# Performer attention and a GEGLU block on one core: the maximum of the k rows as a factor on v instead of a subtraction, and the k projection as row-tiled pairs

## The chip, the cores and the metric

One core of one Trainium2 chip runs the whole program. The metric is device microseconds of one execution. The kernel before took 423.97 us (median of 3 runs, 422.4 to 424.92).

Names used below: PE is the matrix engine, DVE the vector engine, ACT the scalar (activation) engine, POOL the GpSimd engine, SP the engine that issues most DMA transfers. PSUM is the accumulator memory that PE writes.

## The reference, cut to what matters

There are 64 heads (8 batches of 8), 576 tokens each, 64 wide, and 128 random features. The result of attention goes through a GEGLU feed-forward block (512 to 1536 to 512).

```python
def phi(x):                                   # x: q or k, scaled
    proj = np.einsum('bhsd,md->bhsm', x, omega)
    h = proj - np.sum(x * x, axis=-1, keepdims=True) / 2.0
    h = h - np.max(h, axis=-1, keepdims=True)
    return np.exp(h) / np.sqrt(m)
q_p, k_p = (phi(q_s), phi(k_s))
kv  = np.einsum('bhsm,bhsd->bhmd', k_p, v)
z   = np.sum(k_p, axis=2)
num = np.einsum('bhsm,bhmd->bhsd', q_p, kv)
den = np.einsum('bhsm,bhm->bhs', q_p, z)[..., None] + 1e-06
return num / den
# ... then gelu(x @ w_gate) * (x @ w_val) @ w_out
```

Two facts of this arithmetic matter. The maximum of a q row cancels in num / den (but for the 1e-06), so the kernel leaves it out. The maximum of a k row does not cancel: every k row s is weighted by exp(-max_s) before it is summed over s. That weight may be put on the row of k_p (by a subtraction before the exponential), or on the row of v and of the ones that make z (by a factor). The change goes from the first to the second.

## The kernel before

The batch loop interleaves attention of batch t+1 with the feed-forward work of token block t. Only the parts that the argument touches are shown.

```python
    def load_v(b):                      # two batches ahead; POOL casts fp32 to bf16
        vf = ld.tile([P, H, R * D], F32, name="vf", bufs=1)
        vrf = ld.tile([P, 4, D], F32, name="vrf", bufs=1)
        nc.sync.dma_start(out=vf, in_=v[b, :, :SM, :]...)
        ...
        nc.gpsimd.tensor_copy(ve[:, :, :, :D], vf.rearrange("p h (r d) -> p h r d", r=R))
        ...                             # v_ext / v_rbd: v with a column of ones, two buffers
    def attention(b):
        kT = transpose_main(k_in, "k")  # 16 PE transposes, one DVE copy
        ...
        def k_feat(ps, dst, n):
            nmax = work.tile([P, n, 1], F32, name="nmax", bufs=4)
            nc.vector.reduce_max(nmax, ps, axis=AX, negate=True)
            kd = work.tile([P, n, M], F32, name="kd", bufs=5)
            nc.vector.tensor_add(kd, ps, nmax.broadcast_to((P, n, M)))
            nc.scalar.activation(dst, kd, func=Exp)
        for hp in range(H // 2):
            pk = att_tile([P, 8, M], F32, "pk")
            for i in range(4):          # omega2T: block diagonal, 128 x 256
                nc.tensor.matmul(pk[:, 2 * i:2 * i + 2, :], kT[:, 4 * hp + i, :], omega2T)
            k_feat(pk, k_p[:, 2 * hp:2 * hp + 2]..., 8)
        ...                             # the same for the 64 rest rows: pkr, k_pr
        qT = transpose_main(q_in, "q")
        for hp in range(H // 2):
            pq = att_tile([P, 2, 512], F32, "pq")
            ...                         # two 64-row matmuls of 512 columns
            nc.scalar.activation(q_pT[:, hp]..., pq, func=Exp)
        ...
        kz_ps = att_tile([P, 2, 512], F32, "kz_ps")
        for j in range(4):
            nc.tensor.matmul(kz_ps[...], k_pr[:, j, :], vr[:, j]..., start=True, stop=False)
            ...                         # 8 matmuls k_p x v_ext into the same bank
        kz = work.tile([P, 2, 4 * DP1], BF16, name="kz")
        nc.vector.tensor_copy(kz, kz_ps[:, :, :4 * DP1])
        ...                             # nd = q_p x kz, division, transposes into xT
    with tc.manual_schedule(engines={mybir.EngineType.Activation}):
        attention(0)
        for t in range(N_TOK):
            ...                         # loads of batch t + 2
            if t + 1 < B: attention(t + 1)
            if t > 0: project_out(t - 1)
            gate_val(t)
        project_out(N_TOK - 1)
```

ACT runs in the written order. The other engines' orders are chosen when the program is compiled, and then every engine runs its list strictly in order. PSUM is split: two buffers of two banks ("att") for all attention results, four of one bank ("mo") for the feed-forward.

The softmax here doesn't subtract the row's maximum and nothing guards it: scores larger than these inputs give would overflow.

## Time and profile before

| | before |
|---|---|
| span of the profiled run | 422.2 us |
| PE, DVE, ACT, POOL busy | 89%, 59%, 37%, 15% |
| start, until the k transposes of the third batch | 92.7 us |
| six steady iterations (92.69 to 344.59 us, each from its first k transpose to the next's) | 251.9 us, 41.85 to 42.46 us each; the last ends at the first o_ps matmul |
| tail without attention | 77.6 us |

The page's first and fourth parts: busy time with its share of the span and the number of instructions, and the chain of work that ended last, by engine.

```profile
PE 373.9 (89%) x2518; PEld 193.2 (46%) x2561; DVE 249.7 (59%) x380; ACT 154.6 (37%) x202; POOL 62.9 (15%) x87
PE 74%; ACT 9%; DVE 8%; DMA 4%; issue 2%; POOL 1%; SPq 0%; DVEq 0%; POOLq 0%
```

PE holds three quarters of the chain, so what counts is whether PE works and whether it waits. Next, groups of instructions of the kernel before: line, engine, operation, output<-inputs, shapes, count | busy us, mean ns of one | idle time just before them and what ended it.

```profile
L194 DVE TENSOR_REDUCE nmax<-pk 128x8 f32<-128x1024 f32 x32 | 37.6, 1217 | 4.2 <-PE pk L202 4.2
L196 DVE TENSOR_TENSOR kd<-pk,nmax 128x1024 f32<-128x1024 f32 x32 | 37.5, 1213 | 0.0
L197 ACT ACTIVATE k_p<-kd 128x1024 bf16<-128x1024 f32 x32 | 33.8, 1057 | 91.3 <-DVE kd L196 90.1
L202 PE MATMUL pk<-omega2T,kT 128*128 128x256 bf16 x128 | 19.8, 292 | 5.0 <-DVE kd L196 4.9
L104 POOL CAST v_ext_70<-vf 128x2048 bf16<-128x2048 f32 x4 | 7.6, 1892 | 0.6 <-DMA vf<-in_v_dram 0.4
```

The third line is tempting: ACT stood idle for 90 us ahead of the k exponential, waiting for the subtraction. But in the steady iterations PE fills that time with feed-forward matmuls (pk waits for DVE only 5 us in the whole run), so shortening it saves little directly. The last line is, beside the building of the identity matrix at the start, the only kind of arithmetic that POOL does in this kernel: a cast with one input, 1.89 us for 2048 elements per partition, done before anyone needs it.

The first and the last steady iteration in the windows view: the stretch, its length, busy time and count of PE, weight loads, DVE, ACT, POOL, then granted PE clock, DMA share and GB/s.

```profile
92.69:134.64 41.95, 41.01 (x299) 21.15 (x303) 29.51 (x44) 18.75 (x25) 6.95 (x9) 1.00 0.42 82
302.74:344.59 41.85, 40.65 (x297) 21.17 (x302) 29.17 (x44) 18.70 (x24) 0.00 (x0) 1.00 0.09 26
```

And PE in order of time where kz starts in the first of them (start, duration, instruction, count, idle time before it with its releaser):

```profile
111.95 0.59 PE L303 MATMUL v_ps<-xT,w_val_sb 128*128 128x512 bf16 x2
112.43 0.23 PE L231 MATMUL kz_ps<-v_rbd_72,k_pr 128*128 128x130 bf16 x1
...
114.82 0.38 PE L297 MATMUL g_ps<-xT,w_gate_sb 128*128 128x512 bf16 x1 [0.53 <-ACT g_gelu L300]
```

kz starts 19.7 us after the iteration's first k transpose, without any wait; shortly after it PE stands for 0.5 us, because ACT is still busy and no PSUM bank of the feed-forward is free.

### The profile page before, as it was taken

The page shows a single profiled execution, that of the slowest core. Times are in us where ns is not written, and L with a number is a line of the kernel's source. Part 1 is how long each engine was busy: PE and PEld are TensorE (multiplying, and loading weights), DVE is VectorE, ACT ScalarE, POOL GpSimd, SP SyncE. Part 2 cuts the span into 40 slices and gives each one's busy share as a digit, 9 for nine tenths or more (in the row PEclk, how much of TensorE's full clock was granted, in tenths as well). Part 3 has the DMA queues.
Part 4 walks back from the last instruction along what each step waited for, and adds up shares of the span by engine and source line. Part 5 has one row for each costly group of instructions (what it writes and reads, how often), then busy time and mean ns, then how long its engine had stood idle before and what let it go on. Part 6 is the DMA issues. An engine that isn't in the chain of part 4 may idle for free.

```text
span 422.2 us, 6222 instructions
## 1 busy us (share of the span) xinstructions
PE 373.9 (89%) x2518; PEld 193.2 (46%) x2561; DVE 249.7 (59%) x380; ACT 154.6 (37%) x202; POOL 62.9 (15%) x87
## 2 busy tenths in 40 slices
PE   0456847999999999998999999999999999999995
PEld 0224524555455545554555455545554544444442
DVE  1482593649574957495749574957595632433331
ACT  1043046243724362446243624472347221321320
POOL 7563523002301230112011300000000000000000
PEclk9999975999999999999999999999999999999999
DMA  9999997305730673067306600030003003003004
GB/s 179 233 224 207 204 225 85 104 0 64 150 113 2 62 152 112 0 64 149 113 0 64 151 0 3 0 102 2 0 2 99 2 2 100 0 2 99 0 8 93
DMA packets 48444, 33.46 MB, mean 79 GB/s; under 512 B 14624, under 2 KB 43808, under 8 KB 48416
## 3 DMA queue, kind: packets, MB, share of 16 engines
q0 software_dynamic: 30096, 14.16, 26.6%
q1 hardware_dynamic: 18320, 18.91, 15.4%
q8 instruction: 20, 0.33, 0.3%
q14 instruction: 8, 0.07, 0.0%
HBM read 37.78 MB, written 9.44 MB: 112 GB/s over the span
## 4 chain that ended last, share of the span: by engine, by line
PE 74%; ACT 9%; DVE 8%; DMA 4%; issue 2%; POOL 1%; SPq 0%; DVEq 0%; POOLq 0%
PE g_ps L297 21%; PE o_ps L327 20%; PE v_ps L303 19%; ACT q_pT L219 6%; DVE nmax L194 3%; DMA q_rest<-in_q_dram 3%; DVE kd L196 3%; PE pk L202 3%; PE nd L250 2%; PE qT_ps L169 2%; PE xt_ps L261 2%; PE kT_ps L169 2%; ACT L300 2%; DMA out_dram<-o_sb 1%; PE kz_ps L235 1%
## 5 line engine op out<-in xcount | busy, mean ns | idle before, releaser
L297 PE MATMUL g_ps<-xT,w_gate_sb 128*128 128x512 bf16 x422 | 115.7, 383 | 4.1 <-ACT g_gelu L300 2.5
L305 DVE TENSOR_TENSOR gated<-g_gelu,v_ps 128x512 bf16<-128x512 bf16 x108 | 73.7, 682 | 72.5 <-PE v_ps L303 65.7
L300 ACT ACTIVATE g_gelu<-g_ps 128x512 bf16<-128x512 f32 x108 | 63.7, 597 | 143.3 <-PE g_ps L297 138.4
L303 PE MATMUL v_ps<-xT,w_val_sb 128*128 128x512 bf16 x414 | 113.0, 382 | 2.4 <-DVE o_sb L330 1.2
L327 PE MATMUL o_ps<-w_out_sb,gated 128*128 128x512 bf16 x417 | 98.2, 379 | 0.7
L197 ACT ACTIVATE k_p<-kd 128x1024 bf16<-128x1024 f32 x32 | 33.8, 1057 | 91.3 <-DVE kd L196 90.1
L303 PEld LDWEIGHTS <-w_val_sb 128*128 128x128 bf16 x432 | 41.1, 99 | 49.1 <-issue 7.0
L327 PEld LDWEIGHTS <-gated 128*128 128x128 bf16 x432 | 41.8, 98 | 43.0
L297 PEld LDWEIGHTS <-w_gate_sb 128*128 128x128 bf16 x432 | 40.9, 98 | 42.7 <-issue 2.5
L330 DVE COPY o_sb<-o_ps 128x512 f32<-128x512 f32 x36 | 24.0, 683 | 29.2 <-PE o_ps L327 20.7
L194 DVE TENSOR_REDUCE nmax<-pk 128x8 f32<-128x1024 f32 x32 | 37.6, 1217 | 4.2 <-PE pk L202 4.2
L196 DVE TENSOR_TENSOR kd<-pk,nmax 128x1024 f32<-128x1024 f32 x32 | 37.5, 1213 | 0.0
L219 ACT ACTIVATE q_pT<-pq 128x1024 bf16<-128x1024 f32 x32 | 30.2, 1030 | 11.5 <-PE pq L217 11.5
L239 DVE CAST kz<-kz_ps 128x520 bf16<-128x520 f32 x8 | 5.6, 699 | 33.8 <-PE kz_ps L235 33.8
L202 PE MATMUL pk<-omega2T,kT 128*128 128x256 bf16 x128 | 19.8, 292 | 5.0 <-DVE kd L196 4.9
L255 DVE TENSOR_TENSOR x_sb<-nd,iden 128x512 bf16<-128x512 f32 x32 | 22.0, 688 | 0.6
L71 POOL DMA_DIRECT2D k_in<-in_k_dram x8 | 7.2, 906 | 79.5 <-PE rT_ps L182 78.5
L202 PEld LDWEIGHTS <-kT 128*128 128x128 bf16 x128 | 11.5, 103 | 14.7 <-DVE kd L196 11.3
L217 PE MATMUL pq<-qT,omegaT_111 64*128 64x512 bf16 x64 | 12.9, 436 | 5.5 <-DVE qT L172 2.6
L250 PEld LDWEIGHTS <-q_pT 128*128 128x128 bf16 x256 | 12.0, 104 | 9.0 <-issue 6.0
L161 DVE COPY xT<-xt_ps 128x1024 bf16<-128x1024 bf16 (+3 forms) x22 | 11.4, 543 | 6.1 <-PE xt_ps L261 5.7
L250 PE MATMUL nd<-kz,q_pT 128*128 128x65 bf16 x256 | 13.3, 203 | 1.5 <-DVE kz L239 1.0
(66 smaller groups left out, 260.1 us busy)
## 6 DMA issues: line engine op xcount, KB each, us to landing
vf<-in_v_dram SPq DMA_DIRECT2D x8, 1024.0 KB, 5.8
out_dram<-o_sb SPq DMA_DIRECT2D x40, 128.0 KB, 2.4
k_in<-in_k_dram POOLq DMA_DIRECT2D x8, 512.0 KB, 7.9
q_in<-in_q_dram POOLq DMA_DIRECT2D x8, 512.0 KB, 7.5
out_dram<-o_sb SPq DMA_DIRECT2D x16, 256.0 KB, 2.5
w_gate_sb<-in_moe_w_gate_dram POOLq DMA_DIRECT2D x3, 512.0 KB, 14.9
w_val_sb<-in_moe_w_val_dram POOLq DMA_DIRECT2D x3, 512.0 KB, 14.1
w_out_sb<-in_moe_w_out_dram POOLq DMA_DIRECT2D x3, 512.0 KB, 19.4
```

What stands on the lines that cost most here:

```text
L194: nc.vector.reduce_max(nmax, ps, axis=AX, negate=True)
L196: nc.vector.tensor_add(kd, ps, nmax.broadcast_to((P, n, M)))
L197: nc.scalar.activation(dst, kd, func=Exp)
L202: nc.tensor.matmul(pk[:, 2 * i:2 * i + 2, :], kT[:, 4 * hp + i, :], omega2T)
L219: nc.scalar.activation(q_pT[:, hp].rearrange("m a c p -> m a (c p)"), pq, func=Exp)
L250: nc.tensor.matmul(nd[:, h // 4, (h % 4) * DP1:(h % 4 + 1) * DP1], q_pT[:, h // 2, r2, 2 * (h % 2) + rp, :], kz_h(h))
L297: nc.tensor.matmul(g_ps, w_gate_sb[:, jm, fs], xT[:, jm, :], start=(jm == 0), stop=(jm == N_DM - 1))
L300: nc.scalar.activation(g_gelu, g_ps, func=Gelu)
L303: nc.tensor.matmul(v_ps, w_val_sb[:, jm, fs], xT[:, jm, :], start=(jm == 0), stop=(jm == N_DM - 1))
L305: nc.vector.tensor_mul(gated[:, jf, :], g_gelu, v_ps)
L327: nc.tensor.matmul(o_ps, gated[:, jf, qq * P:(qq + 1) * P], w_out_sb[:, jf, :], start=(jf == 0), stop=(jf == N_DFF - 1))
L330: nc.vector.tensor_copy(o_sb, o_ps)
```

## The change

Its intent: take the subtraction from DVE and let the k exponential read PSUM at once, without waiting for the maximum. The maximum is exponentiated separately (128 x 36 values) and multiplied into v and the ones on POOL. The k projection becomes pairs of matmuls with 64 rows each, which use the two halves of the array, in place of one matmul against a half-empty block-diagonal matrix. The fp32 tiles of v get a second buffer, because they now live until the multiply.

```diff
-        vf = ld.tile([P, H, R * D], F32, name="vf", bufs=1)
-        vrf = ld.tile([P, 4, D], F32, name="vrf", bufs=1)
+        vf = ld.tile([P, H, R * D], F32, name="vf")          # the pool's 2 buffers
+        vrf = ld.tile([P, 4, D], F32, name="vrf")
...
-        nc.gpsimd.tensor_copy(ve[:, :, :, :D], vf.rearrange(...))   # and two for the rest rows
...
-        def k_feat(ps, dst, n): ...    # reduce_max, tensor_add, exponential
         for hp in range(H // 2):
-            pk = att_tile([P, 8, M], F32, "pk")
+            pk = att_tile([P, 2, 4, M], F32, "pk")
             for i in range(4):
-                nc.tensor.matmul(pk[:, 2 * i:2 * i + 2, :], kT[:, 4 * hp + i, :], omega2T)
-            k_feat(pk, ...)
+                for r2 in range(2):
+                    sl = slice(r2 * D, (r2 + 1) * D)
+                    nc.tensor.matmul(pk[:, r2, i, :], kT[sl, 4 * hp + i, :], omegaT2[sl])
+            nc.scalar.activation(k_p[:, hp]..., pk..., func=Exp)
+            nc.vector.reduce_max(nmax[:, :, 4 * hp:4 * hp + 4], pk, axis=AX, negate=True)
...
         for hp in range(H // 2):       # q features
             ...
             nc.scalar.activation(q_pT[:, hp]..., pq, func=Exp)
+            if hp == 0:
+                wk = work.tile([P, 2, 18], F32, name="wk")
+                nc.scalar.activation(wk, nmax, func=Exp)
...
+        for hh in range(2):
+            isl = slice(8 * hh, 8 * hh + 8)
+            nc.gpsimd.tensor_mul(vei[:, isl, :, :D], vfi[:, isl],
+                                 wki[:, isl].unsqueeze(3).broadcast_to((P, 8, 2, D)))
+        nc.gpsimd.tensor_copy(vei[:, :, :, D], wki[:, :16])
+        for e in range(2):
+            ...                         # the rest rows: one multiply, one copy each
         kz_ps = att_tile([P, 2, 512], F32, "kz_ps")
```

The cut part re-indexes k_p and k_pr for the new order of rows.

More of the change, by code (lines that the diff above doesn't have):

```diff
@@ L88 @@
         nc.vector.memset(v_rbd[i], 0.0)
-        nc.vector.memset(v_ext[i][:, :, :, D:DP1], 1.0)
-        for e in range(2):
-            nc.vector.memset(v_rbd[i][e * SR:(e + 1) * SR, :, e, D:DP1], 1.0)
     def load_v(b):
-        vf = ld.tile([P, H, R * D], F32, name="vf", bufs=1)
-        vrf = ld.tile([P, 4, D], F32, name="vrf", bufs=1)
+        vf = ld.tile([P, H, R * D], F32, name="vf")
+        vrf = ld.tile([P, 4, D], F32, name="vrf")
         nc.sync.dma_start(
@@ L102, in load_v @@
                     .rearrange("j s d -> s j d"))
-        ve, vr = v_ext[b % 2], v_rbd[b % 2]
-        nc.gpsimd.tensor_copy(ve[:, :, :, :D],
-                              vf.rearrange("p h (r d) -> p h r d", r=R))
-        for e in range(2):
-            sl = slice(e * SR, (e + 1) * SR)
-            nc.gpsimd.tensor_copy(vr[sl, :, e, :D], vrf[sl])
-        return ve, vr
+        return vf, vrf
     omega_f = singles.tile([M, D], F32)
@@ L122 @@
     omegaT2 = singles.tile([2 * D, M], BF16)
-    omega2T = singles.tile([2 * D, 2 * M], BF16)
-    nc.vector.memset(omega2T, 0.0)
     for e in range(2):
@@ L127 @@
         nc.vector.tensor_copy(omegaT2[sl], omegaT_ps)
-        nc.vector.tensor_copy(omega2T[sl, e * M:(e + 1) * M], omegaT_ps)
     w_gate_sb = singles.tile([P, N_DM, d_ff], BF16)
@@ L176, in attention @@
         k_in, k_rest, q_in, q_rest = kq.pop(b)
-        ve, vr = vx.pop(b)
+        vf, vrf = vx.pop(b)
+        ve, vr = v_ext[b % 2], v_rbd[b % 2]
         kT = transpose_main(k_in, "k")
@@ L186, in attention @@
         nc.vector.tensor_copy(rT, rT_ps)
-        k_p = work.tile([P, H, R, M], BF16, name="k_p")
-        k_pr = work.tile([P, 4, M], BF16, name="k_pr")
-        def k_feat(ps, dst, n):
-            nmax = work.tile([P, n, 1], F32, name="nmax", bufs=4)
-            nc.vector.reduce_max(nmax, ps, axis=AX, negate=True)
-            kd = work.tile([P, n, M], F32, name="kd", bufs=5)
-            nc.vector.tensor_add(kd, ps, nmax.broadcast_to((P, n, M)))
-            nc.scalar.activation(dst, kd, func=Exp)
+        k_p = work.tile([P, H // 2, 2, 4, M], BF16, name="k_p")
+        k_pr = work.tile([P, 2, 2, M], BF16, name="k_pr")
+        nmax = work.tile([P, 2, 18], F32, name="nmax")
         for hp in range(H // 2):
-            pk = att_tile([P, 8, M], F32, "pk")
+            pk = att_tile([P, 2, 4, M], F32, "pk")
             for i in range(4):
-                nc.tensor.matmul(pk[:, 2 * i:2 * i + 2, :], kT[:, 4 * hp + i, :], omega2T)
-            k_feat(pk, k_p[:, 2 * hp:2 * hp + 2].rearrange("p h r m -> p (h r) m"), 8)
-        pkr = att_tile([P, 4, M], F32, "pkr")
-        for jj in range(2):
-            nc.tensor.matmul(pkr[:, 2 * jj:2 * jj + 2, :], rT[:, jj, :], omega2T)
-        k_feat(pkr, k_pr, 4)
+                for r2 in range(2):
+                    sl = slice(r2 * D, (r2 + 1) * D)
+                    nc.tensor.matmul(pk[:, r2, i, :], kT[sl, 4 * hp + i, :], omegaT2[sl])
+            nc.scalar.activation(k_p[:, hp].rearrange("p a i m -> p a (i m)"),
+                                 pk.rearrange("p a i m -> p a (i m)"), func=Exp)
+            nc.vector.reduce_max(nmax[:, :, 4 * hp:4 * hp + 4], pk, axis=AX, negate=True)
+        pkr = att_tile([P, 2, 4, M], F32, "pkr")
+        for jj in range(2):
+            for j2 in range(2):
+                sl = slice(j2 * D, (j2 + 1) * D)
+                nc.tensor.matmul(pkr[:, j2, jj, :], rT[sl, jj, :], omegaT2[sl])
+        nc.scalar.activation(k_pr, pkr[:, :, :2], func=Exp)
+        nc.vector.reduce_max(nmax[:, :, 16:], pkr[:, :, :2], axis=AX, negate=True)
         qT = transpose_main(q_in, "q")
@@ L225, in attention @@
         nc.scalar.activation(q_pTr.rearrange("m a c p -> m a (c p)"), pqr[:, :, :256], func=Exp)
+        vei = ve.rearrange("p h (c r) d -> p (h c) r d", r=2)
+        vfi = vf.rearrange("p h (c r d) -> p (h c) r d", c=2, r=2)
+        wki = wk.rearrange("p r i -> p i r")
+        for hh in range(2):
[4 more added lines that the diff above has]
+        for e in range(2):
+            sl = slice(e * SR, (e + 1) * SR)
+            vre = vr[sl, :, e, :].rearrange("p (a j) d -> p a j d", j=2)
+            nc.gpsimd.tensor_mul(vre[..., :D],
+                                 vrf[sl].rearrange("p (a j) d -> p a j d", j=2),
+                                 wki[sl, 16:].unsqueeze(3).broadcast_to((SR, 2, 2, D)))
+            nc.gpsimd.tensor_copy(vre[..., D], wki[sl, 16:])
         kz_ps = att_tile([P, 2, 512], F32, "kz_ps")
@@ L230, in attention @@
             g, c0 = j // 2, (j % 2) * 2 * DP1
-            nc.tensor.matmul(kz_ps[:, g, c0:c0 + 2 * DP1], k_pr[:, j, :],
+            nc.tensor.matmul(kz_ps[:, g, c0:c0 + 2 * DP1], k_pr[:, j % 2, j // 2, :],
                              vr[:, j].rearrange("p e c -> p (e c)"), start=True, stop=False)
@@ L235, in attention @@
                     nc.tensor.matmul(kz_ps[:, g, c0 + e * DP1:c0 + (e + 1) * DP1],
-                                     k_p[:, 2 * j + e, r, :], ve[:, 2 * j + e, r, :],
+                                     k_p[:, j, r % 2, 2 * e + r // 2, :], ve[:, 2 * j + e, r, :],
                                      start=False, stop=(e == 1 and r == R - 1))
```

## The prediction

> **What bounds it now.** The page: span 422.2 us, PE 89% busy, DVE 59%, ACT 37%, POOL 15%. PE holds 74% of the chain that ended last. Three stages: a start (0 to 71 us) in which attention 0 and 1 run one after the other with PE often idle; six steady iterations of 42.0 us (92.85 to 344.75 in the chain); a 77 us tail without attention, which the change leaves alone. A steady iteration is 144 feed-forward matmuls at 0.216 us (31 us), about 8.5 us of attention matmuls, and about 2 us of PE waits. The page puts idle of 90 us on the k exponential, "waiting for DVE kd", but ACT is off the critical path there: PE fills that time with o_ps matmuls.
>
> **Removed.** Per batch DVE loses the subtraction: 4 x 1.21 + 0.68 = 5.5 us (33 to 36% of its k phase and copies). The k exponential reads PSUM directly and runs beside the reduction, so the k phase, serial on DVE, shrinks from about 10.5 us to 5.2 us. POOL loses its casts (1.89 + 2 x 0.40 us), which ran ahead of need.
>
> **Moved.** k projection: 18 matmuls of 256 columns at 0.108 us become 18 row-tiled pairs of 128 columns. The pq pairs show that two 64-row matmuls share the time of one (four take 0.54 us), but also about 0.1 us around a group; the Trainium skill (TensorEngine Tiling (Array Packing), Key Properties) says that changing the tiling mode drains the engine. Net PE: 0 to -0.5 us per batch, no more.
>
> **Added.** POOL must now multiply v by exp(-max) after the exponential of the max, and before any kz matmul, since the first kz matmul reads the v rest that POOL writes last. The trace has only one-input casts on POOL (0.92 ns per element). The Trainium skill (GPSIMD Engine Reference, section 3.1) puts a two-input operation at about 2.6 cycles per element, 4497 ns for 2048. My estimate from it: 2 x 2.3 + 2 x 0.6 + three small copies at 0.2 = 6.3 us. No run shows it yet.
>
> **On the critical path.** Steady state, counted from the k transposes. Now kz starts at 19.7 us. After: PE work puts pq at about 13.0 us, the first q exponential ends at 14.2, the small exponential at 14.4, POOL at about 20.7. The compiled order of PE places only 5 gate/value matmuls before kz, against 14 now, so PE should stand about 3.5 us in front of kz, and the 9 matmuls (1.9 us) come later. The later waits (about 1 us) vanish. Sum: +2.2 us per iteration, 13 us for six. Start: about 5 us saved per k phase, given back by 6.3 us of POOL after the first q exponential; in attention 0 POOL is also held by weight transfers issued ahead of it (until 33 us now). Net about +1 us (-3 to +4).
>
> **Predicted**: 436 us, range 424 to 447. Faster by over 2%: 5%; within 2%: 29%; slower: 66%.
>
> **What would show it.** Windows of one iteration: length about 44.2 us; DVE falling by about 5.5 us, ACT unchanged, POOL rising from about 6.9 to about 10.5 us. Waits: PE or its weight loads at kz waiting for POOL's v_rbd, about 3.5 us in each iteration; POOL multiply of 128x1024 at about 2.3 us. pk groups on PE no dearer than before.
>
> **What would make it wrong.** POOL multiplying at the cast's rate (about 1 us per 1024): its chain would be 3.3 us, kz no longer late, and the kernel about 1% faster. POOL slower than estimated, or the granted clock falling after each stand of 3 to 4 us: 450 us. The start gaining its full 5 us per attention: 5 to 8 us less.

## The result, and the profile after

The changed kernel took 443.32 us (median of 4 runs, 440.86 to 446.52) beside 423.36 us for the kernel before (4 runs). The ratio is 1.0472, with a 95% interval of 1.038 to 1.0564: slower. A ratio here is the mean time of one kernel's fast runs over that of the other's fast runs of the same rounds, so it is not quite the ratio of the medians. The four runs fall in two pairs, near 441 us (granted clock 0.965) and near 446 us (0.953 and 0.954); the profiled one, of 446.52 us, is of the second kind.

The same two parts of the page, after:

```profile
PE 377.6 (85%) x2660; PEld 193.4 (43%) x2705; DVE 210.4 (47%) x331; ACT 154.0 (35%) x210; POOL 85.5 (19%) x119
PE 21%; issue 9%; POOL 1%; DVE 0%; POOLq 0%
```

The second line warns of the chain view: it covers only a third of the span. The chain runs back from the last instruction to a POOL multiply, and there it is lost: the profile does not see what POOL waited for and calls it "issue". The waits view says the same:

```profile
POOL v_ext_71 L226 <- issue: 45.5, 4, 39.5
PE kz_ps L241 <- POOL v_rbd_73 L235: 11.9, 4, 3.4
PE kz_ps L241 <- POOL v_rbd_72 L235: 11.8, 4, 3.4
DVE nmax L190 <- ACT k_p L188: 4.3, 4, 2.0
```

(Columns: us in total, times, the longest.) What POOL waits for there is ACT, which writes the small exponential wk: in the iteration shown below wk ends at 108.84 us and the multiply starts at 108.98. "issue" hides that. The second and third lines are new and certain: at kz, eight times out of eight, PE waits for POOL, 23.7 us in all.

The groups after:

```profile
L190 DVE TENSOR_REDUCE nmax<-pk 128x8 f32<-128x1024 f32 x32 | 37.6, 1217 | 4.3 <-ACT k_p L188 4.3
L188 ACT ACTIVATE k_p<-pk 128x1024 bf16<-128x1024 f32 x32 | 31.9, 1022 | 62.4 <-PE pk L187 61.9
L187 PE MATMUL pk<-omegaT_102,kT 64*128 64x128 bf16 x256 | 12.3, 228 | 3.6 <-DVE nmax L190 3.6
L226 POOL TENSOR_TENSOR v_ext_71<-vf,wk 128x1024 bf16<-128x1024 f32 x8 | 15.3, 1928 | 45.5 <-issue 45.5
```

The subtraction is gone. POOL's multiply takes 1.93 us for 1024 elements, as long as its cast took for 2048. Here is what that does to one iteration: first POOL, then PE, in order of time.

```profile
108.98 3.82 POOL L226 TENSOR_TENSOR v_ext_70<-vf,wk 128x1024 bf16<-128x1024 f32 x2 [1.96 <-issue]
112.75 0.32 POOL L228 CAST v_ext_70<-wk 128x32 bf16<-128x32 f32 x1
112.92 0.61 POOL L232 TENSOR_TENSOR v_rbd_72<-vrf,wk 64x256 bf16<-64x256 f32 x1
...
114.32 0.20 POOL L235 CAST v_rbd_72<-wk 64x4 bf16<-64x4 f32 x1
```

```profile
111.38 0.38 PE L313 MATMUL v_ps<-xT,w_val_sb 128*128 128x512 bf16 x1
114.57 0.27 PE L241 MATMUL kz_ps<-v_rbd_72,k_pr 128*128 128x130 bf16 x1 [2.81 <-POOL v_rbd_72 L235]
```

PE has nothing left that stands ahead of kz in its order, and stands for 2.8 us until POOL's last small copy is done (POOL's chain is 5.5 us). The order chosen when the program is compiled has a part in this: it puts 5 feed-forward matmuls of the new token block ahead of kz, where the kernel before had 14. That iteration and the last of the six, in the windows view (columns as before):

```profile
94.17:140.69 46.52, 43.02 (x317) 21.96 (x320) 24.63 (x39) 18.69 (x26) 9.79 (x13) 0.93 0.39 75
323.19:367.10 43.91, 40.34 (x315) 20.29 (x320) 24.56 (x39) 18.64 (x25) 5.46 (x7) 1.00 0.09 25
```

Both hold the same work of PE, DVE and ACT and the same wait of 2.8 us (POOL issues no more loads in the last), but the first is 2.6 us longer, and its clock is 0.93. In narrow windows around kz one sees when the clock falls; the last line is the iteration that kept it:

```profile
111.60:114.57 2.97, 0.16 (x1) 0.10 (x1) 0.00 (x0) 2.35 (x3) 2.84 (x6) 0.82 0.45 132
114.57:117.00 2.43, 2.35 (x36) 2.29 (x37) 0.04 (x1) 0.00 (x0) 0.00 (x0) 0.50 0.89 271
117.00:119.00 2.00, 1.85 (x14) 1.01 (x14) 1.35 (x2) 0.00 (x0) 0.00 (x0) 0.50 1.05 333
119.00:121.00 2.00, 2.00 (x18) 1.05 (x15) 1.57 (x4) 0.29 (x1) 0.00 (x0) 0.67 0.07 11
121.00:123.00 2.00, 2.00 (x24) 1.27 (x22) 1.19 (x2) 0.31 (x1) 0.00 (x0) 1.00 0.00 0
343.56:346.00 2.44, 2.44 (x47) 1.78 (x47) 0.96 (x2) 0.00 (x0) 0.00 (x0) 1.00 0.00 0
```

Here the clock drops to half while PE stands, and it is back at full only some 6 us after work has begun again (between 119 and 121 us). In two of the other iterations it falls a moment after the stand (0.2 and 0.3 us). In the trace's clock record the five stretches at half clock of these iterations last 6.8, 3.4, 6.8, 3.4 and 3.4 us, whole multiples of 3.41. The Trainium skill (TensorE: Matmul & The Clock Gate, "What's actually happening") describes such a gate: PE is granted 4 of 8 clock pulses when it was idle, and all of them after a window of activity; the window runs freely, so the moment differs from run to run. The trace agrees in kind: half the clock, and one iteration that was spared.

So the 22.5 us between the two profiled spans divide like this:

| part | before | after | difference | how |
|---|---|---|---|---|
| start, until the k transposes of the third batch | 92.69 | 94.17 | +1.5 us | start times |
| six iterations, if all were as long as the one at clock 1.00 | 251.90 | 6 x 43.91 = 263.46 | +11.6 us | stand at kz, less what the change saves |
| the rest of the six iterations | - | 272.93 - 263.46 | +9.5 us | slow clock after the stand |
| tail | 77.61 | 77.60 | 0.0 us | start times |

(272.93 us is 367.10 - 94.17.) The stretches at half clock make 23.9 us together; half of that, 11.9 us, is the most that they can cost, and the 9.5 us lie below it. All this was at first only a reading of two traces. The experiments test it.

### The profile page after: what moved, and what is told of

Its sections match the earlier page's. It is cut to its first block, busy times and chain, and to the rows that moved or that the text cites. A ratio compares the mean times of both kernels' runs of the same rounds, so it can differ in the third digit from the quotient of the medians.

```text
span 444.7 us, 6524 instructions
## 1 busy us (share of the span) xinstructions
PE 377.6 (85%) x2660; PEld 193.4 (43%) x2705; DVE 210.4 (47%) x331; ACT 154.0 (35%) x210; POOL 85.5 (19%) x119
## 5 line engine op out<-in xcount | busy, mean ns | idle before, releaser
L313 PE MATMUL v_ps<-xT,w_val_sb 128*128 128x512 bf16 x417 | 115.3, 386 | 1.7 <-issue 1.1
L337 PE MATMUL o_ps<-w_out_sb,gated 128*128 128x512 bf16 x417 | 99.6, 380 | 1.4 <-issue 1.0
L337 PEld LDWEIGHTS <-gated 128*128 128x128 bf16 x432 | 38.8, 98 | 46.0 <-issue 3.9
L188 ACT ACTIVATE k_p<-pk 128x1024 bf16<-128x1024 f32 x32 | 31.9, 1022 | 62.4 <-PE pk L187 61.9
L245 PEld LDWEIGHTS <-k_p 128*128 128x128 bf16 x256 | 16.3, 128 | 22.6 <-issue 22.6
L226 POOL TENSOR_TENSOR v_ext_71<-vf,wk 128x1024 bf16<-128x1024 f32 x8 | 15.3, 1928 | 45.5 <-issue 45.5
L226 POOL TENSOR_TENSOR v_ext_70<-vf,wk 128x1024 bf16<-128x1024 f32 x8 | 15.3, 1931 | 43.8 <-issue 43.8
L260 PE MATMUL nd<-kz,q_pT 128*128 128x65 bf16 x256 | 14.2, 210 | 1.5 <-DVE kz L249 1.2
L187 PE MATMUL pk<-omegaT_102,kT 64*128 64x128 bf16 x256 | 12.3, 228 | 3.6 <-DVE nmax L190 3.6
```

Source lines behind the costliest of these rows:

```text
L188: nc.scalar.activation(k_p[:, hp].rearrange("p a i m -> p a (i m)"), pk.rearrange("p a i m -> p a (i m)"), func=Exp)
L226: nc.gpsimd.tensor_mul(vei[:, isl, :, :D], vfi[:, isl], wki[:, isl].unsqueeze(3).broadcast_to((P, 8, 2, D)))
L260: nc.tensor.matmul(nd[:, h // 4, (h % 4) * DP1:(h % 4 + 1) * DP1], q_pT[:, h // 2, r2, 2 * (h % 2) + rp, :], kz_h(h))
L313: nc.tensor.matmul(v_ps, w_val_sb[:, jm, fs], xT[:, jm, :], start=(jm == 0), stop=(jm == N_DM - 1))
L337: nc.tensor.matmul(o_ps, gated[:, jf, qq * P:(qq + 1) * P], w_out_sb[:, jf, :], start=(jf == 0), stop=(jf == N_DFF - 1))
```

## The experiments

Theory: (a) PE waits at kz for POOL, because the multiply has become the last link between the maxima and kz; (b) the wait itself is worth about 2.1 us per iteration (43.91 against 41.85 us in its counterpart; this is net of what the change saves), and (c) the slow clock after it another 1.6 us on the average in the profiled run (9.5 / 6; the expectations say 8.7 us in all, from an end of the last iteration that was read 0.16 us too late). Rivals: the row-tiled pairs are dear, because the array must change its tiling mode around each group; or the exponential and the reduction, which now read the same PSUM tile, hinder each other; or the clock has another cause than the stand (the bursts of DMA in the lines above fall into the same moments). Each kernel that was meant to be correct gave the right result. Times are medians of 4 to 6 runs, beside the kernel before on the same chip.

### Only the wait removed

```diff
-        nc.gpsimd.tensor_mul(vei..., vfi..., wki...)   # and the other five POOL operations
+        # load_v casts v to bf16 ahead of need, as in the kernel before; wk is computed and not used
```

> The changed kernel, but v is cast to bf16 on POOL ahead of need, as in the kernel before, and is not multiplied by exp(-max); the reductions and the small exponential stay, unused. Wrong result on purpose (the weights of the k rows are missing). The order of PE in a steady iteration is the same as in the changed kernel, so only the wait of kz for POOL is taken away. Theory (kz waits for the POOL chain, and the stand of PE lets its clock fall): no wait on POOL at kz, granted clock 1.00 in all six steady iterations, about 41.3 us each instead of 44.1 to 46.6; kz earlier by about 3.4 us in each of the first two attentions; total about 413 us. Rival (the row-tiled pairs and their changes of tiling mode, or the exponential and the reduction reading the same PSUM tile, cost the time): still 436 us or more.

Measured: 411.69 us against 421.91, ratio 0.9763 (0.9733 to 0.9792). The result is wrong (relative error 0.19). Two of its steady iterations:

```profile
83.88:125.11 41.23, 40.71 (x316) 20.09 (x320) 24.50 (x39) 18.68 (x26) 6.95 (x9) 1.00 0.43 84
207.60:248.76 41.16, 40.38 (x315) 20.14 (x320) 24.55 (x39) 18.70 (x26) 6.94 (x9) 1.00 0.35 55
```

The order of PE (checked by its weight loads in all six iterations), the pairs, the reductions and the exponentials are those of the changed kernel, and the loss is gone: 41.2 us at full clock instead of 43.9 to 46.6. Both rivals that blame the pairs or PSUM fall. It also shows what the stand costs before any saving is taken off: 43.91 less 41.2, 2.7 us per iteration, nearly its whole length. One caveat: this kernel has one buffer for the fp32 v tiles, like the kernel before, so its iterations are a clean comparison but its start is not. Its gain of 2.4% is therefore not what the change alone would have brought without the multiply: the last experiment puts the single buffer at 4.6 us, which leaves about 1.3% (an estimate, since that was measured on another version).

### The two halves of the change, one at a time

Row-tiled pairs alone, in the kernel before:

```diff
-                nc.tensor.matmul(pk[:, 2 * i:2 * i + 2, :], kT[:, 4 * hp + i, :], omega2T)
+                for r2 in range(2):
+                    sl = slice(r2 * D, (r2 + 1) * D)
+                    nc.tensor.matmul(pk[:, 4 * r2 + i, :], kT[sl, 4 * hp + i, :], omegaT2[sl])
```

> The kernel before with only the row-tiled pairs for the k projection; subtraction, casts of v and all else as before. Theory: pairs cost PE about 0.1 us less per group of four than the 256-column matmuls (0.33 against 0.45 us), so 420.5 to 423.5 us, within 1% of before. Rival (changes of tiling mode are what makes the changed kernel slow): 430 us or more.

Measured: 419.55 us (418.75 to 420.41) against 421.91, ratio 0.995 (0.9917 to 0.9982): within 2%, but faster, and a little below the expected range. The pairs are no loss. In the steady state a group of four pairs holds PE for 0.33 us where four 256-column matmuls held it for 0.45 us (from the start of its first matmul to the start of the next work, in the two traces). The Trainium skill (TensorEngine Tiling (Array Packing), Key Properties) says that a change of tiling mode drains the array. The 0.33 us do not hold all of that: the first pair starts 0.31 us after the o_ps matmul ahead of it in the changed kernel, against 0.22 us for the first 256-column matmul in the next experiment, which changes no mode there. Counted from that o_ps matmul, a group of four takes 0.64 us as pairs and 0.65 us as 256-column matmuls, so it gains almost nothing; the larger gain lies in the groups of eight (0.87 against 1.09 us).

The factor alone, with the k projection of the kernel before:

```diff
-                for r2 in range(2):
-                    sl = slice(r2 * D, (r2 + 1) * D)
-                    nc.tensor.matmul(pk[:, r2, i, :], kT[sl, 4 * hp + i, :], omegaT2[sl])
+                nc.tensor.matmul(pk[:, i, :, :], kT[:, 4 * hp + i, :], omega2T)
```

> The changed kernel with the k projection of the kernel before: 18 full-height matmuls of 256 columns per batch in place of 18 row-tiled pairs; the factor, the direct exponential and the POOL multiply stay. Theory: the factor alone makes the loss; PE has about 0.4 us more work per iteration ahead of the first q exponential, so POOL starts that much later: 1 to 4 us above the changed kernel, 442 to 448 us, with the same stand of about 2.8 us at kz. Rival (the pairs carry the loss): near 424 us.

Measured: 444.66 us (442.33 to 444.81) against 422.1, ratio 1.051 (1.046 to 1.056). The factor carries the whole loss. Its compiled order has 6 feed-forward matmuls ahead of kz in place of 5, and the stand is as long. PE at kz in one iteration:

```profile
113.54 0.22 PE L239 MATMUL kz_ps<-v_rbd,k_pr 128*128 128x130 bf16 x1 [2.73 <-POOL v_rbd L233]
```

### The stand filled, to keep the clock

```diff
         kz_ps = att_tile([P, 2, 512], F32, "kz_ps")
+        for _ in range(12):
+            nc.tensor.matmul(kz_ps[:, 0, :], ident, qT[:, :4, :])   # overwritten by kz
```

> The changed kernel with 12 dummy matmuls of 512 columns put on PE just before kz, into the tile that kz then overwrites (same result). They fill the stand of 2.8 us without shortening it. Theory (two costs: the wait itself, about 2.1 us per iteration against before, and on top of it the slow clock that follows an idle PE, 1.0 to 2.5 us per iteration, 8.7 us in the profiled run): granted clock 1.00 in the steady iterations, each 44.1 to 44.5 us, total about 438 us in spite of up to 2 us more in each of the first two attentions, where dummies run at the slow clock; and the runs lie closer together than 440.9 to 446.5. Rival (the slow clock has another cause than PE's stand, or costs nothing): unchanged or slower, 444 to 452 us.

Measured: 436.22 us (435.43 to 438.14) against 421.91, ratio 1.0333 (1.0301 to 1.0364). Two steady iterations:

```profile
94.87:138.89 44.02, 43.16 (x328) 21.41 (x332) 24.49 (x39) 18.69 (x26) 9.78 (x13) 1.00 0.41 78
182.92:226.94 44.02, 43.16 (x328) 21.40 (x333) 24.43 (x38) 18.69 (x26) 9.78 (x13) 1.00 0.41 78
```

This separates (b) from (c). Useless work on PE, which cannot make kz come any sooner, lowers the ratio from 1.0472 to 1.0333, about 6 us: the iterations are 44.0 us, within 0.1 us of the one iteration of the changed kernel that kept its clock, and the clock is 1.00. So the slow clock follows from the stand. The DMA of these iterations is that of the changed kernel (share 0.41 against 0.39), so its bursts do not pull the clock down. 6 us is less than the 9.5 us of the table because the profiled run was the slowest of four, 3 us above the median, and because the start was 0.7 us longer here. With the clock kept, the kernel is still 3.3% slower than before.

With 4 dummies instead of 12, PE still stands for 1.9 us:

> As the version with 12 dummy matmuls ahead of kz, but with 4, so that PE still stands for about 1.9 us of the 2.8 us in each iteration. If a stand of 1.9 us is too short to let the clock fall: granted clock 1.00 in the six steady iterations, 43.9 to 44.1 us each, total 436 to 438 us, as with 12. If the clock falls at such a stand too: some iterations of 45 to 46.6 us at a clock of 0.93 to 0.96, total 439 to 446 us.

Measured: 437.7 us (436.97 to 438.35) against 421.82, ratio 1.0371 (1.0345 to 1.0398). The total fits the first of the two outcomes that were expected (the highest run lies 0.35 us above its range), but the clock did fall once, which belongs to the second. Five of the six iterations kept the clock (43.9 to 44.0 us), but in the sixth it fell, after a stand of no more than this:

```profile
333.02 0.22 PE L243 MATMUL kz_ps<-v_rbd,k_pr 128*128 128x130 bf16 x1 [1.90 <-POOL v_rbd L235]
```

```profile
330.00:333.00 3.00, 1.12 (x6) 0.39 (x4) 0.00 (x0) 2.42 (x4) 2.91 (x6) 1.00 0.38 87
335.00:337.00 2.00, 2.00 (x14) 0.95 (x13) 1.31 (x2) 0.00 (x0) 0.00 (x0) 0.51 0.03 8
```

In one profile of each kernel, then, the clock fell in 5 of 6 iterations with a stand of 2.8 us, in 4 of 6 with 2.7 us (the factor alone), in 1 of 6 with 1.9 us, and in none with the 0.5 us of the kernel before. That it differs between equal iterations fits the freely running window of the skill's page, and the traces say more. In every trace the clock changes only at times that lie whole multiples of 3.41 us apart, so these times mark a grid of windows. Four windows of this grid from the profiled run of the changed kernel, around the first two stands (after which the clock fell) and the last (after which it did not):

```profile
110.08:113.49 3.41, 1.68 (x9) 0.53 (x8) 0.57 (x1) 3.38 (x5) 3.41 (x5) 1.00 0.89 170
157.87:161.28 3.41, 0.60 (x8) 0.28 (x7) 0.00 (x0) 2.60 (x4) 3.09 (x6) 1.00 0.52 139
338.77:342.19 3.42, 1.85 (x9) 0.62 (x10) 0.69 (x1) 3.40 (x5) 3.42 (x4) 1.00 0.42 97
342.19:345.60 3.41, 2.04 (x40) 1.56 (x39) 0.58 (x1) 0.79 (x2) 1.26 (x4) 1.00 0.00 0
```

The stand of the last iteration was split between two windows, so that PE was busy for 54% and 60% of them; in the first two it was busy for 49% and 18%. Over the 18 steady iterations of the changed kernel, of the factor alone and of the 4 dummies, PE was busy for 18 to 49% of the window in all ten windows after which the clock fell. In those that kept the clock it was busy for 54% or more, but for one at 45% (4 dummies). So in these runs it is how much of a window the stand takes that counts, and not its length alone; the exception stays open (busy PE is modelled in these traces, and some records can be missing). The DMA share does not divide the two kinds: 0.20 to 0.89 in the ten, 0.00 to 1.13 in the others.

### The chain started earlier

```diff
         nc.vector.reduce_max(nmax[:, :, 16:], pkr[:, :, :2], axis=AX, negate=True)
+        wk = work.tile([P, 2, 18], F32, name="wk")
+        nc.scalar.activation(wk, nmax, func=Exp)
...
-            if hp == 0:
-                wk = work.tile([P, 2, 18], F32, name="wk")
-                nc.scalar.activation(wk, nmax, func=Exp)
```

> The changed kernel with one move: the small exponential of the maxima is issued on ACT before the q exponentials, right after the reduction of the rest rows, instead of behind the first q exponential. All work stays. Theory: POOL starts about 3.2 us earlier in a steady iteration and is done before PE reaches kz; no stand, clock 1.00, about 41.3 us per iteration; in the first attention POOL is still held by weight transfers, in the second it gains up to 3 us; total about 417 us, faster than before by about 1.5%. Rival (the cost is in the pairs or in PSUM contention): no gain, about 443 us.

Measured: 415.48 us (414.68 to 416.67) against 421.91, ratio 0.9857 (0.9825 to 0.9889): faster than before by 1.4%, which is within the 2% mark but clear of 1, from one moved instruction. The last POOL instruction and kz in one iteration:

```profile
105.22 0.20 POOL L234 CAST v_rbd<-wk 64x4 bf16<-64x4 f32 x1
```

```profile
104.93 0.82 PE L306 MATMUL g_ps<-xT,w_gate_sb 128*128 128x512 bf16 x3
105.63 0.23 PE L240 MATMUL kz_ps<-v_rbd,k_pr 128*128 128x130 bf16 x1
```

POOL is done just before PE gets there, all work is the same (PE's order differs in a few places; 4 feed-forward matmuls stand ahead of kz), and nothing waits. An iteration takes 41.1 to 41.2 us at clock 1.00:

```profile
129.48:170.68 41.20, 40.42 (x315) 20.27 (x320) 24.50 (x39) 18.81 (x26) 9.70 (x13) 1.00 0.46 84
```

So POOL's slow multiply costs nothing in itself; it costs when it starts too late for its length.

### The chain on DVE

```diff
-            nc.gpsimd.tensor_mul(vei..., vfi..., wki...)    # and the copies: all six POOL operations
+            nc.vector.tensor_mul(vei..., vfi..., wki...)
```

> The changed kernel with the multiply of v and its small copies on DVE in place of POOL, at the same place behind the first q exponential. DVE gave up 5.5 us of subtraction and stands idle for 6.3 us before kz. Theory: DVE's chain takes about 3.5 us (two 128x1024 at 1.2 us, two 64x256 at 0.4, three small copies) against 5.6 us on POOL, so kz comes about 2 us earlier: a stand of 0.5 to 1 us, too short to let the clock fall; 41.5 to 42 us per iteration, total 416 to 420 us. If instead any chain behind the first q exponential is too late, or DVE's other work is pushed back, 425 us or more.

Measured: 414.93 us (413.74 to 415.27) against 422.1, ratio 0.981 (0.9758 to 0.9862; the interval crosses the 2% mark), somewhat better than expected. With wk left in its late place, DVE does the same work in 3.4 us (102.87 to 106.26 us in one iteration of its trace), and kz comes 18.15 us after the first k transpose, against 20.4. PE stands for 0.1 us there (0.5 to 1 was expected); the compiled order has 7 feed-forward matmuls ahead of kz in this version. A shorter chain thus does as well as an earlier one. The multiply:

```profile
L226 DVE TENSOR_TENSOR v_ext<-vf,wk 128x1024 bf16<-128x1024 f32 x16 | 18.9, 1225 | 10.9 <-ACT wk L213 10.9
```

Here the profile does name ACT's wk as the releaser, which supports the reading of "issue" above.

### The start: the first multiply, and the second buffer of v

In the version with the early wk, the first kz still came at 36.4 us, because POOL first had to issue weight transfers, held in turn by the landing of earlier transfers. So the first batch's multiply was put on DVE:

```diff
+        eng = nc.vector if b == 0 else nc.gpsimd
-            nc.gpsimd.tensor_mul(...)
+            eng.tensor_mul(...)
```

> The version with the early small exponential (415.5 us), with the multiply of the first attention only on DVE, where POOL is held by weight transfers issued ahead of it (kz of the first attention came at 36.4 us there, against 31.7 us where POOL has no multiply). Theory: kz of the first attention comes at about 33.5 us, and all later work moves forward by as much: 412 to 414 us. If something else then holds the second attention (the arrival of its k), 415 us.

Measured: 412.55 us (412.45 to 413.88) against 422.1, ratio 0.9772 (0.9735 to 0.9809), and the first kz at 33.81 us, as expected. The interval reaches across the 2% mark but is clear of 1.

In all kernels with two buffers for the fp32 v tiles, the first q rest rows arrived later (18.3 to 19.3 us) than in those with one (16.6 to 17.1 us). The last pair of runs undoes that part of the change, beside the same version unchanged:

```diff
-        vf = ld.tile([P, H, R * D], F32, name="vf")
+        vf = ld.tile([P, H, R * D], F32, name="vf", bufs=1)      # vrf likewise
```

> The version with the early small exponential and the first multiply on DVE (412.5 us), with one buffer for the fp32 v tiles, as the kernel before has, in place of two. With two, the second batch's v is issued at 3.1 us, beside the first q, and the first q rest arrives at 18.3 to 19.3 us; with one, v waits, and in the three one-buffer kernels seen q rest arrived at 16.6 to 17.1 us. Theory (the second buffer delays the start): q rest at about 16.7 us, the first kz at about 32 us instead of 33.8, total 410.5 to 411.5 us. Rival (the arrival has another cause, or the later v then comes too late for the second attention): q rest unchanged, or a wait of the second multiply for v; 412 us or more.

> The same version with two buffers again, unchanged, on the same chip and beside the same runs of before: 412 to 414 us, first q rest at 18.3 to 19.3 us.

Measured, beside 421.94 us for the kernel before: 408.6 us (408.13 to 409.47) with one buffer, ratio 0.9685 (0.9659 to 0.9711), and 413.19 us (412.66 to 413.69) with two, ratio 0.9788 (0.9762 to 0.9813). The gain of 4.6 us is more than twice what was expected (410.5 to 411.5 us in total, from about 412.5). PE at the arrival of the first q rest, with two buffers and with one:

```profile
18.26 0.37 PE L172 MATMUL rT_ps<-ident,q_rest 128*128 128x128 bf16 x2 [4.33 <-DMA q_rest<-in_q_dram]
```

```profile
14.08 0.37 PE L172 MATMUL rT_ps<-ident,q_rest 128*128 128x128 bf16 x2 [1.55 <-DMA q_rest<-in_q_dram]
```

With two buffers the second batch's v is issued at 3.1 us and competes with the first k and q; with one it is issued at 25.9 us, when the first multiply has freed the tile, and still comes early enough (the second kz moves from 62.97 to 58.75 us). The earlier kernels with one buffer lie between: there a cast freed the tile sooner, the second v was issued at 8.9 to 9.2 us, and the q rest arrived at 16.6 to 17.1 us. So over these three groups, twelve traces in all, the later second v goes with the earlier q rest; the expectation was taken from the middle group. This version, the changed kernel with an early wk, the first multiply on DVE and one buffer for v, beats both kernels: 3.2% faster than before.

## Why the prediction was right or wrong

The direction, the main mechanism (the wait at kz) and the range were right: 443.3 us lies in 424 to 447, and "slower" had two chances in three. The middle, 436 us, was 7 us low, and for a reason: the sum had no term for the clock.

- **The wait at kz.** Predicted: kz about 20.7 us into an iteration, a stand of about 3.5 us, 5 matmuls of the feed-forward ahead of it, +2.2 us per iteration, length 44.2. Measured: 20.4 us, 2.8 us, and 43.91 us in the iteration at full clock, +2.1 over the 41.85 of its counterpart. The wait was right, and it was read from two things: the data dependence (the first kz matmul needs what POOL writes last) and the compiled order of PE. That the sum of 2.2 us came out so close is partly luck: the stand was 0.7 us shorter than predicted, but of the later waits, which were to vanish and give back about 1 us, only 0.4 went (PE's other idle time is 0.8 us in that iteration, 41.85 - 40.65 = 1.2 us in its counterpart).
- **POOL's time.** Predicted 6.3 us, worked out from the figure of the Trainium skill (GPSIMD Engine Reference, section 3.1). Measured 5.5 us: 1.93 us for 1024 elements instead of 2.3, 0.61 us for 256, as predicted, small copies of 0.2 to 0.3 us. Had the one-input rate of the trace been used instead (0.92 ns per element), the wait would have been missed: the prediction itself gives a chain of 3.3 us for it and no wait, and the version with a chain of 3.4 us on DVE did stand for only 0.1 us.
- **The term that was missing.** The sum "+2.2 us per iteration, 13 us for six" left the granted clock at 1.00. "the granted clock falling after each stand of 3 to 4 us" stood only among the things that could go wrong. It fell after stands of 2.8 us, in five of six iterations of the profiled run, and cost 9.5 us there (about 6 us on the average of the runs, by the filled stand). With it the sum for the profiled run is 13 + 1 + 9.5 = 23.5 us, and the two profiled spans differ by 22.5. The range held the result because it was wide, not because this term was in it: for a falling clock the prediction names 450 us, which is outside.
- **The k phase.** Predicted to shrink from 10.5 to 5.2 us per attention, with the exponential beside the reduction. In the compiled program each reduction waits for the exponential of the same tile (the line of waits above, ACT k_p), so the two are staggered: in the first attention, 7.1 us (20.22 to 27.30) against 10.6 (18.33 to 28.89). In the steady state that was worth nothing directly, as predicted.
- **The start.** Predicted +1 us, from savings of 5 us per k phase given back on POOL. Measured +1.5 us, by other terms: the first q rest came 2.2 us later, and saving and loss within each attention about cancelled (the path from q rest to the first kz went from 18.3 to 18.0 us). The effect of the second buffer of v was not foreseen; that it costs time was shown only in the last pair of runs, on a better version.
- **Row-tiled pairs.** Predicted 0 to -0.5 us of PE per batch. Measured about -0.2 us for a group of eight and almost nothing for a group of four, and -0.5% for the pairs alone (about 2 us, or 0.3 per batch). Right, with the 0.1 us around a group that it named.
- **Busy times.** DVE fell by 4.9 us per iteration (29.51 to 24.63), not 5.5: means of single instructions count the overlap of neighbours twice (two such operations in a row took 2.35 us, not 2.43). ACT stayed at 18.7. POOL rose to 9.8, not 10.5.

What stays open: why one window with PE busy for 45% kept its clock; how much of the stand is owed to the compiled order of PE (the nine feed-forward matmuls that now come after kz, 1.9 us at 0.216 us each, could have filled most of it; no run kept POOL's chain with the old order); and how the 2.2 us in the changed kernel's own start divide between the second buffer and the differences from run to run.

## What to carry to other kernels

When work is moved from a busy engine to an idle one, ask first who waits for the result: a chain that is off the critical path while it runs ahead of need can become the critical path when it gets a late input and a consumer that stands in a fixed order. Start such a chain at the first moment at which its input exists; here one moved instruction turned 4.7% slower into 1.4% faster. And cost a new stand of PE at more than its length, because the clock that follows it may be half for several microseconds (3.4 or 6.8 us here).

## What the Trainium skill lacked or had wrong

- GPSIMD Engine Reference, section 3.1, gives about 2.6 cycles per element for an operation with two inputs (4497 ns for 2048 elements). In these runs the multiply of fp32 v by a broadcast factor into bf16 took 1.93 us for 1024 elements (1.88 ns per element) and two in a row took 3.82 us, about 15% less. DVE took 1.225 us for the same operation, a factor of 1.57, where the page has 1.96. (The page's operation is an addition, in fp32 throughout as far as it says; and spans on POOL are rough in the profile.)
- TensorE: Matmul & The Clock Gate, "What's actually happening" and "Why this matters for your kernels", names an idle window of about 3.4 us, and advises no idle gaps over about 3 us. Here the clock fell at stands of 2.8 us (5 of 6 iterations), 2.7 us (4 of 6) and 1.9 us (1 of 6). A gap under 3 us was not safe here. Nor need the window be idle throughout: the clock changed on a grid of 3.41 us, which agrees with the page, but it fell after windows in which PE was busy for 18 to 49%.
- TensorEngine Tiling (Array Packing), Key Properties, says that a change of tiling mode drains the array, without a figure. Here the first of the 64-row pairs started 0.31 us after a 128-row matmul of 512 columns, where without a change of mode the next matmul started 0.22 us after it: about 0.1 us for the change into the pairs. With it, a group of four pairs of 128 columns took 0.64 us, against 0.65 us for four 256-column matmuls of the same work.
- No page that was used here says that a second buffer can cost time by letting a transfer start too early: it moved the first q rest from 14.1 to 18.3 us and the total from 408.6 to 413.2 us.
